# Small blocks without their low copies, constant products and spread search steps at the second layer's beginning, and the fallback branch moved forward

## The chip, the cores and the metric

The kernel runs on one core of a Trainium2 chip. The metric is the device time of one execution in microseconds (us). The core has TensorE (PE in the tables, with its weight loads as PEld), VectorE (DVE), ScalarE (ACT), GpSimd (POOL) and SyncE (SP, which issues most DMAs). Each engine works through its own instructions in order; semaphores hold an instruction back until what it needs is there.

## The reference

Three layers follow each other (cut to what is computed):

```python
# attention: B=4, H=12, S=448, D=64, causal
scores = mask(q @ k.T / 8); attn = softmax(scores); x = attn @ v      # x: 1792 x 768
# _moe_ref: 8 experts, hidden 1024
e = argmax(x @ w_gate); y = gate * (relu(x @ w1[e]) @ w2[e])          # any number of tokens per expert
# _moe2_ref: the same sizes, but each expert takes exactly 1792 / 8 = 224 tokens
for idx in argsort(-logits.flatten()):                                # best (token, expert) pair first
    tok, e = divmod(idx, 8)
    if assigned[tok] < 0 and counts[e] < 224:
        assigned[tok] = e; counts[e] += 1
out[mask_e] = relu(y[mask_e] @ w1[e]) @ w2[e]
```

## The kernel before

Products in float32 accuracy are made of three products of rounded parts: high by high, low by high and high by low (names ending in `h` and `l`: `w1h`, `w1l`, `xh`, `xl`, `hh`, `hl`). ACT rounds a weight tile from its raw buffer to the high part, and another engine subtracts it to get the low part; this pair is `split`, at L171 and L172 in the first layer and L773 and L774 in the second. A raw buffer comes free, and the next load of weights is issued, when both have read it.

`moe1` takes each expert's tokens in blocks of 128. A last block of at most 64 tokens is computed by `small` (L305): its 64 tokens fill half of the 128 columns, the other half of `xh` gets the low parts of the same tokens by two DVE copies (L309), and one product with `w1h` (L316) then makes high by high and low by high at once; a second one of 64 columns adds high by low. The branches of `expert` (L381, L389, L400, L403) decide at run time which blocks there are; all engines take them, each for itself, and `hint` names the target ahead of some of them. L417 is a row of constant products, ahead of the first expert: their operands are constants and nothing reads their result. The layer's tail (L445 to L474) brings the logits of the second layer's gate into place and sets up the first search.

`moe2` assigns the tokens with `search(p)`, one expert after the other. A search tests 40 thresholds at once in four rounds. In one round DVE compares all tokens with the thresholds (L622), PE counts by 14 small products (L665), DVE judges the counts (L666, L668), PE adds the judgments up (L676), and DVE sets the next thresholds from them (L677). After the last round PE makes a total (L566), `assign` numbers the tokens with PE's help (L710, L725, L729), and the numbers go to POOL, which gathers the tokens by an indirect DMA (L781). The generator `gen` holds these steps and yields ahead of each product of PE, so other work can be put between them: `go(n)` runs n steps, `turn` runs one when it is due, `finish` runs all that are left.

For each expert `take` transposes the gathered tokens on PE (L800) and ACT and DVE make `xh` and `xl` of them (L803, L804). The up product (L815) makes eight tiles `f` of the hidden layer from six chunks `k`, the down product (L838) makes the outputs, ACT copies them (L841), and POOL stores them by indirect DMAs (L785, the last two L791). In the first expert the up product for the first four `f` is made chunk by chunk as the weights come (`up4`, L822), so that twelve products follow each step pair of the search for the second expert.

At the very end DVE compares `bad` with zero (L918), every engine loads the verdict into a register (L921) and branches on it (L922). The body behind the branch computes the layer again by another assignment, for inputs that the search can't settle. It isn't entered with these inputs.

Of the kernel before, what the change touches and what calls it, by code (L numbers as in the profile page):

```python
# [119 lines left out]
def moe1(tc, w1, w2, wg, xs, y2, l2, ident, before, iob, cr, gt, g0, raw, early, iok, L, srch):  # L120
    nc = tc.nc
    with ExitStack() as c:
# [319 lines left out]
        for e in range(E):  # L442
            expert(e)

# [25 lines left out]
        tail3(False)  # L470
        V.tensor_mul(rh.rearrange("p (i e) -> p i e", e=E), oi[:, :, None].to_broadcast([128, NB, E]),
                     l2c[:, None, :].to_broadcast([128, NB, E]))
        nc.tensor.matmul(pU[1][:, :NB * E], hp, rh, start=True, stop=True)
        V.tensor_add(L, L, pU[1][:, :NB * E].rearrange("p (i e) -> p i e", e=E))  # L474


def moe2(tc, w1, w2, y2, out, ident, before, ones, io8, iok, iob16, L, srch, raw, force):
# [7 lines left out]
    with ExitStack() as c:  # L485
# [50 lines left out]
        iob = io8[:, None, :].to_broadcast([128, PT, E])  # L536

# [87 lines left out]
        def search(p):  # L625
# [32 lines left out]
            for r in range(RN):  # L658
# [5 lines left out]
                for i in range(PT):  # L664
                    nc.tensor.matmul(t[:TH], T["g"][:, i, :TH], T["oh"][:, i], start=(i == 0), stop=(i == PT - 1))  # L665
                V.tensor_tensor_reduce(T["d"][:TH], t[:TH], T["capm"][:TH], scale=1.0, scalar=-3.0e38,  # L666
                                       op0=OP.subtract, op1=OP.max, accum_out=T["mx"][:TH])
                V.tensor_scalar(T["ok"][:TH], T["mx"][:TH], 0.0, None, op0=OP.is_ge)  # L668
# [7 lines left out]
                nc.tensor.matmul(t[:, :1], ones[:TH], T["ok"][:TH], start=True, stop=True)  # L676
                V.scalar_tensor_tensor(thr, t[:, :1].to_broadcast([128, TH]), steps[:, r:r + 1], T["base"], op0=OP.mult,  # L677
# [9 lines left out]
            t = total()  # L687

# [6 lines left out]
        def assign(p):  # L695
# [14 lines left out]
            nc.tensor.matmul(t[:, :1], before, T["rt"], start=True, stop=True)  # L710
            V.tensor_copy(T["col"], t[:, :1])
# [14 lines left out]
            V.tensor_scalar(T["ev"], t[:16, :NA], float(N), None, op0=OP.min)  # L726
            yield YY[9]
# [38 lines left out]
        def split(p, k):  # L766
# [7 lines left out]
            (nc.gpsimd if p == 0 and k >= KD and k % 2 else V).tensor_sub(l, r, h.bitcast(F32))  # L774
# [20 lines left out]

        def take(kk):
            t = ps.tile([128, 512], F32, name="w", bufs=6)[:, :2 * CAP].rearrange("p (k g t) -> p k g t", k=2, g=2)
# [10 lines left out]
        def up(f, h):  # L808
            if h == 0:
                U[f] = ps.tile([128, 512], F32, name="w", bufs=6)[:, :CAP]  # L810
# [6 lines left out]
        def up4(k):  # L817
            for f in range(4):
                if k == 0:
                    U[f] = ps.tile([128, 512], F32, name="w", bufs=6)[:, :CAP]  # L820
# [11 lines left out]
        def down(g, hf, f0, f1):  # L832
            if f0 == 0:
                Y[0] = ps.tile([128, 512], F32, name="w", bufs=6)[:G2, :384]
# [19 lines left out]

        go(1)
        split(0, 0)
        go(2)
        split(0, 1)
        for kk in range(0, KD, 2):
            take(kk)  # L860
        for k in range(KD):
            go(2 if k < 3 else 1)
            if k + 2 < KD:
                split(0, k + 2)
            up4(k)
        for f in range(4, KF):
# [7 lines left out]
            split(0, KD + f)  # L874
        for p in range(E):
            early = p > 0 and p + 1 in done
            if p:
# [3 lines left out]
                for f in range(KF):  # L881
# [3 lines left out]
                    turn(p, 1)  # L885
                    relu(f)
# [3 lines left out]
            for g in range(2):  # L890
                for hf in range(2):
                    for f in range(0, KF, 2):
                        down(g, hf, f, f + 2)
                        turn(p, 1)
                        if n == s0[0]:
                            finish(p + 1)
                            flush()
                        if p + 1 in done and not early:
# [15 lines left out]
                if p < E - 1 or g == 0:  # L914
                    put(p, g)


        V.tensor_scalar(T["bi"], bad, 0.0, None, op0=OP.not_equal)  # L918
        if force:
            V.memset(T["bi"], 1)  # L920
        again = nc.values_load(T["bi"][0:1, 0:1], min_val=0, max_val=1)  # L921
        with tc.If(again > 0):  # L922
            reset()
            for p in range(E):
                best()
                V.tensor_tensor(T["eq"], T["lm"], T["m"][:, :, None].to_broadcast([128, PT, E]), op=OP.is_equal)
                V.tensor_mul(T["eq"], T["eq"], iob)
                V.tensor_reduce(T["mn"], T["eq"], axis=AX.X, op=OP.min)
                V.tensor_tensor(T["oh"], iob, T["mn"][:, :, None].to_broadcast([128, PT, E]), op=OP.is_equal)
                exact()  # L930
                owned()
                V.scalar_tensor_tensor(apen, T["asg"], -BIG, apen, op0=OP.mult, op1=OP.add)
                V.memset(T["fl"], 0.0)
                V.scalar_tensor_tensor(T["full"], cap, 0.0, left, op0=OP.is_equal, op1=OP.mult)
                for _ in assign(p):
                    pass
                gather(p)
                pend.clear()
                for k in range(NC):
                    load(p, k)  # L940
                    r = raw[(p * NC + k) % NR]
                    if k < KD:
                        h, l = w1h[:, k], w1l[:, k]
                    else:
                        r, h, l = r[:, :DM], w2h[:, k - KD], w2l[:, k - KD]
                    A.activation(h, r, AF.Copy)
                    V.tensor_sub(l, r, h.bitcast(F32))
                for kk in range(0, KD, 2):
                    take(kk)
# [346 lines left out]
```

## Time and profile before

| | us |
|---|---|
| median of three runs | 988.75 (986.0 to 988.78) |
| profiled execution | 990.98 |
| its span, first to last instruction | 989.1 |
| PE, DVE, ACT, POOL busy | 891.8, 629.1, 503.1, 215.4 |
| first to second layer | about 625 to 655 |
| first expert of the second layer | about 655 to 715 |
| experts two to eight | about 715 to 966 (PE busy 37.22 us of 715.5 to 753, 24.90 of the 24.90 from 941) |
| end | 966 to 989.1 |

The span is the time from the first to the last instruction of the profiled execution; 1.9 us lie around it. The mean granted clock of TensorE over the span is 0.945 of 2.4 GHz. An engine's busy time counts neither its waits nor its branches and semaphores, so a busy PE at a low granted clock is slow without waiting. A row of a timeline has in brackets how long the engine was idle ahead of it and what it waited for. A name like "PE w L838" is an instruction by engine, written tile and line.

### The profile page before, as it was taken

To read this page: it belongs to the slowest core of one execution; us is meant where nothing else is said; L and a number is where in the kernel's file an instruction comes from. 1 tells how busy PE (TensorE), PEld (TensorE's weight loads), DVE (VectorE), ACT (ScalarE), POOL (GpSimd) and SP (SyncE) were. 2 spreads that over 40 slices of the span, in tenths; PEclk is the share of its full clock that TensorE was granted. 3 is DMA by queue.
4 is the path that set the end of the run, shared out by engine and by line. 5 is a ranking of instruction groups with operands and counts; after the bars stand their busy time and mean duration, and the time that the engine had idled before them with its cause. 6 is when DMAs were issued, how large, how long until landed. Compare 5 with 4: busy or idle time off the path is not lost. (4 is left out here: it accounts for less than half of the span.)

```text
span 989.1 us, 18118 instructions
## 1 busy us (share of the span) xinstructions
PE 891.8 (90%) x6122; PEld 744.1 (75%) x6122; DVE 629.1 (64%) x1815; ACT 503.1 (51%) x1101; POOL 215.4 (22%) x244
## 2 busy tenths in 40 slices
PE   5999999995899996987999999458999999999993
PEld 3666666663778885766798878348899999999993
DVE  6888989868552613853821152578797887975640
ACT  5888888854563524654822253033444444445540
POOL 5555444404121111111211112104111011011001
PEclk9999999996999998998999999757999999999997
DMA  8654555706743803873831031074685766766701
GB/s 174 132 148 118 144 138 119 251 11 206 269 146 132 305 34 103 289 290 112 301 152 49 33 101 50 22 244 139 188 246 171 218 190 182 222 199 199 256 16 31
DMA packets 76911, 156.54 MB, mean 158 GB/s; under 512 B 30753, under 2 KB 41793, under 8 KB 76738
## 3 DMA queue, kind: packets, MB, share of 16 engines
q1 hardware_dynamic: 70514, 128.44, 42.2%
q0 software_dynamic: 6224, 26.11, 8.1%
q8 instruction: 70, 1.15, 0.5%
q14 instruction: 103, 0.84, 0.3%
HBM read 135.84 MB, written 18.67 MB: 156 GB/s over the span
## 5 line engine op out<-in xcount | busy, mean ns | idle before, releaser
L202 PE MATMUL pU<-w1h,xx 128*128 128x512 f32 x336 | 120.8, 414 | 9.0 <-DVE xx L256 2.9
L1037 ACT ACTIVATE p<-p,nm 112x112 f32<-112x112 f32 x192 | 99.8, 522 | 14.5 <-DVE nm L1030 14.2
L815 PE MATMUL w<-xh,w1h 128*128 128x224 f32 x360 | 102.1, 284 | 0.0
L815 PE MATMUL w<-xl,w1h 128*128 128x224 f32 x360 | 99.2, 276 | 0.3 <-DVE xl L804 0.3
L815 PE MATMUL w<-xh,w1l 128*128 128x224 f32 x360 | 98.8, 275 | 0.0
L1030 DVE CUSTOM_DVE_ANT_0 p<-s,msk 112x112 f32<-112x112 f32 x192 | 83.3, 440 | 12.9 <-PE s L1026 11.7
L838 PE MATMUL w<-w2h,hh 128*112 128x384 f32 x256 | 91.2, 356 | 0.0
L838 PE MATMUL w<-w2h,hl 128*112 128x384 f32 x256 | 88.0, 344 | 0.0
L838 PE MATMUL w<-w2l,hh 128*112 128x384 f32 x256 | 87.7, 342 | 0.3 <-DVE w2l L774 0.3
L202 PEld LDWEIGHTS pU<-w1h,xx 128*128 128x128 f32 x336 | 63.9, 191 | 27.0 <-issue 5.4
L1025 PE MATMUL s<-kh,qs 128*112 128x112 f32 x192 | 73.8, 384 | 10.4 <-DVE kh L1013 6.1
L1046 PE MATMUL t<-ident,p 112*112 112x112 f32 x480 | 80.3, 267 | 1.4 <-ACT pt L1051 0.8
L1008 POOL TENSOR_TENSOR qs<-qr,qs 64x448 fp32r<-64x448 f32 x44 | 54.3, 1253 | 82.4 <-ACT qs L1007 62.9
L815 PEld LDWEIGHTS w<-xl,w1h 128*128 128x128 f32 x360 | 69.1, 192 | 0.5 <-DVE xl L804 0.5
L815 PEld LDWEIGHTS w<-xh,w1h 128*128 128x128 f32 x360 | 69.0, 192 | 0.5
L815 PEld LDWEIGHTS w<-xh,w1l 128*128 128x128 f32 x360 | 69.1, 192 | 0.0
L172 DVE TENSOR_TENSOR w2l<-raw,w2h 128x768 fp32r<-128x768 f32 x64 | 58.2, 953 | 16.8 <-ACT w2h L171 14.5
L202 PE MATMUL pU<-w1l,xx 128*128 128x512 f32 x168 | 67.0, 399 | 0.0
L1057 PE MATMUL o<-pt,vt 112*64 112x336 f32 (+3 forms) x384 | 66.3, 424 | 0.0
L827 ACT ACTIVATE hh<-w 128x224 fp32r<-128x224 f32 x64 | 22.9, 358 | 84.5 <-PE w L815 63.7
L172 DVE TENSOR_TENSOR w1l<-raw,w1h 128x1024 fp32r<-128x1024 f32 x46 | 54.2, 1225 | 18.2 <-ACT w1h L171 13.5
L785 POOL DMA_INDIRECT out_dram<-yo,idx x15 | 15.3, 1021 | 231.2 <-ACT yo L841 203.0
(308 smaller groups left out, 2236.0 us busy)
## 6 DMA issues: line engine op xcount, KB each, us to landing
raw<-in_moe_w_dram SPq DMA_DIRECT2D x96, 512.0 KB
raw<-in_moe_w_dram SPq DMA_DIRECT2D x128, 384.0 KB
kr<-in_k_dram SPq DMA_DIRECT2D x46, 224.0 KB
qr<-in_q_dram SPq DMA_DIRECT2D x24, 224.0 KB
vt<-in_v_dram SPq DMA_DIRECT2D x48, 112.0 KB
xs<-xr SPq DMA_DIRECT2D x4, 1120.0 KB
xs<-xr SPq DMA_DIRECT2D x4, 238.0 KB
kr<-in_k_dram SPq DMA_DIRECT2D x4, 112.0 KB
```

Of the source, the lines that this page charges most:

```text
L172: (on or nc.vector).tensor_sub(l, r, h.bitcast(F32))
L202: nc.tensor.matmul(pU[half], a[:, k], w[:, k, cs], start=(m == 0), stop=(m == 17))
L785: nc.gpsimd.indirect_dma_start(out=out, out_offset=bass.IndirectOffsetOnAxis(ap=idx[p % 3][:, g:g + 1], axis=0), in_=yo[:, g], in_offset=None)
L815: nc.tensor.matmul(u, w[:, k, fs], x[:, k], start=(k == 0 and n == 0), stop=(k == KD - 1 and n == 2))
L827: A.activation(hh[:, f], u, AF.Relu)
L838: nc.tensor.matmul(y, a[:, f, g * G2:(g + 1) * G2], w[:, f, hf * 384:(hf + 1) * 384], start=(f == 0 and n == 0), stop=(f == KF - 1 and n = ...
L1008: (nc.gpsimd if u > 1 else nc.vector).tensor_sub(qs[64:], qr, qs[:64].bitcast(F32))
L1025: nc.tensor.matmul(s[:, :w], QS[u][:, h, i * Q:(i + 1) * Q], KH[u][:, h, :w], start=True, stop=False)
L1030: nc.vector.tensor_tensor_reduce(p, s[:, :w], msk[:, S - w:], scale=-0.125, scalar=3.0e38, op0=OP.add, op1=OP.min, accum_out=nm)
L1037: nc.scalar.activation(p, p, AF.Exp, bias=RS[u, "m"][:, h, i:i + 1], scale=-1.0, accum_out=RS[u][:, h, i:i + 1])
L1046: nc.tensor.transpose(t[:, k], P[u, h][:, o + k * Q:o + (k + 1) * Q], ident[:Q, :Q])
L1057: nc.tensor.matmul(OPS[u][h * 64:(h + 1) * 64, k * Q:], VT[u][:, h, k], PT[u, h][:, k, k * Q:], start=(k == 0), stop=(k == NQ - 1))
```

## The change

Five things are changed.

1. In `small` the two copies at L309 are gone. The columns that they filled stay zero, and the product of the low parts of the tokens with `w1h` is no longer made in these blocks.
2. Constant products, of 128x512 in bfloat16 as those of L417, are put into PE's order: ten in the first layer's tail (2, 2, 2 and 4), 43 in the first search (2 behind each L665, 4, 4, 4 and 5 behind the four L676, 5, 6 and 2 behind L566, L710 and L725) and 28 between there and the first transposes (7, 2, 4, 5 and 10).
3. `up4` is cut into two halves of six products; for the first three chunks a search step runs ahead of each half.
4. The four w2l subtractions of the first expert that POOL made are made by DVE.
5. The verdict is loaded during the down product of the seventh expert (p = 6), with a hint for the branch, and the branch stands in the up product of the eighth, behind its first tile. The body repeats what is needed up to that place, and uses four PSUM buffers of its own (`alt`). At the end there is no branch.

```diff
         def small(e, j):
-            for s in (slice(0, 1), slice(1, KD)):
-                nc.vector.tensor_copy(xh[:, s, HB:], xl[:, s, :HB])
             sp = begin(e, j, gf[:, e + 1:e + 2])
...
+        def warm(n):
+            for _ in range(n):
+                nc.tensor.matmul(wz, before, iob16[:, None, :].to_broadcast([128, 4, 128]), start=True, stop=True)
...
                 V.tensor_tensor_reduce(T["d"][:TH], t[:TH], T["capm"][:TH], scale=1.0, scalar=-3.0e38,
                                        op0=OP.subtract, op1=OP.max, accum_out=T["mx"][:TH])
+                if p == 0:
+                    warm(2)
                 V.tensor_scalar(T["ok"][:TH], T["mx"][:TH], 0.0, None, op0=OP.is_ge)
...
                 nc.tensor.matmul(t[:, :1], ones[:TH], T["ok"][:TH], start=True, stop=True)
+                if p == 0:
+                    warm(4 if r < RN - 1 else 5)
...
-            (nc.gpsimd if p == 0 and k >= KD and k % 2 else V).tensor_sub(l, r, h.bitcast(F32))
+            V.tensor_sub(l, r, h.bitcast(F32))
...
+        warm(7)
         go(1)
+        warm(2)
         split(0, 0)
-        go(2)
+        go(1)
+        warm(4)
+        go(1)
+        warm(5)
         split(0, 1)
+        warm(10)
         for kk in range(0, KD, 2):
             take(kk)
         for k in range(KD):
-            go(2 if k < 3 else 1)
+            go(1)
             if k + 2 < KD:
                 split(0, k + 2)
-            up4(k)
+            up4(k, 0, 2)
+            if k < 3:
+                go(1)
+            up4(k, 2, 4)
...
+        def judge():
+            finish(E - 1)
+            V.tensor_scalar(T["bi"], bad, 0.0, None, op0=OP.not_equal)
...
+            verdict.append(nc.values_load(T["bi"][0:1, 0:1], min_val=0, max_val=1))
+            tc.mark_branch_hint_location("again", verdict[0] > 0, engines=list(nc.engines))
+
+        def redo():
+            u0 = U[0]
+            alt.extend([ps.tile([128, 512], F32, name="w", bufs=6) for _ in range(4)])
+            with tc.If(verdict[0] > 0, label="again"):
+                reset()
...
+                    if last:
+                        U[0] = u0
+                        up(0, 0, True)
+                        up(0, 1, True)
+                        break
...
                     up(f, 1)
                     turn(p, 1)
+                    if p == E - 1 and f == 0:
+                        redo()
                     relu(f)
...
+                        if p == E - 2 and n == 4:
+                            judge()
```

Three places in the order of the engines follow. PE, second layer, from the search to the first half product; w is the PSUM tile of the up product, gp that of the search. Before:

```order
L665 MATMUL gp<-t_oh,t_g 40x8
L676 LDWEIGHTS ones
L676 MATMUL gp<-t_ok,ones 128x1
L822 MATMUL w<-xh,w1h 128x224
L822 MATMUL w<-xh,w1l 128x224
L822 MATMUL w<-xl,w1h 128x224
```

After:

```order
L855 MATMUL w<-xh,w1h 128x224
L855 MATMUL w<-xh,w1l 128x224
L855 MATMUL w<-xl,w1h 128x224
L693 LDWEIGHTS ones
L693 MATMUL gp<-t_ok,ones 128x1
L855 MATMUL w<-xh,w1h 128x224
L855 MATMUL w<-xh,w1l 128x224
L855 MATMUL w<-xl,w1h 128x224
```

L693 is the old L676 and L855 the old L822: six of the twelve products now stand between the counts (L680, the old L665) and L693, and six behind it.

DVE at the same place, from the tokens' low parts (L804) to the second weight subtraction; srch holds the thresholds. Before:

```order
L804 TENSOR_TENSOR xl<-w,xh 128x448 x3
L666 ISA t_d,t_mx<-gp,t_capm 40x8
L666 ISA t_mx 40x1
L668 TENSOR_SCALAR t_ok<-t_mx 40x1
L552 TENSOR_REDUCE t_mn<-t_ao 128x14
L677 SCALAR_TENSOR_TENSOR srch_87<-gp,steps,t_base 128x40
L622 TENSOR_TENSOR t_g<-t_mm,srch_87 128x14x40
L660 TENSOR_TENSOR t_col<-srch_87,steps 128x1
L661 TENSOR_SCALAR t_base<-iok,steps,t_col 128x40
L774 TENSOR_TENSOR w1l<-raw_90,w1h 128x1024
```

After:

```order
L837 TENSOR_TENSOR xl<-w,xh 128x448 x3
L681 ISA t_d,t_mx<-gp,t_capm 40x8
L681 ISA t_mx 40x1
L685 TENSOR_SCALAR t_ok<-t_mx 40x1
L567 TENSOR_REDUCE t_mn<-t_ao 128x14
L799 TENSOR_TENSOR w1l<-raw_90,w1h 128x1024
L696 SCALAR_TENSOR_TENSOR srch_87<-gp,steps,t_base 128x40
L637 TENSOR_TENSOR t_g<-t_mm,srch_87 128x14x40
```

The subtraction of w1l (L799, the old L774) has moved from behind the next thresholds to ahead of them (L696, the old L677).

POOL at the end of the kernel, from the stores of the last expert. Before:

```order
L785 DMA out_dram<-yo,idx_23605 1792x768
L791 DMA out_dram<-yo,idh 3584x384 x2
L921 TENSOR_LOAD t_bi
L922 COMPARE_AND_BRANCH
L608 MEMSET apen 128x14
```

After:

```order
L930 UNCONDITIONAL_BRANCH
L930 ISA
L930 UNCONDITIONAL_BRANCH
L810 DMA out_dram<-yo,idx_23583 1792x768
L816 DMA out_dram<-yo,idh 3584x384 x2
L1356 UNCONDITIONAL_BRANCH
L1356 ISA
```

The load of the verdict and the branch (now L930) stand ahead of the last expert's stores (L810 and L816, the old L785 and L791), and behind the stores only the program's end is left.

## Rows read from the trace of the kernel before

**Rows 1.** Stages: busy time by engine (instructions), granted clock, DMA share, GB/s.
```profile
630.40:646.60 16.20, 4.21 (x77) 3.42 (x77) 12.88 (x68) 0.00 (x0) 0.00 (x0) 0.55 0.11 36
655.10:676.00 20.90, 19.00 (x134) 17.94 (x135) 14.85 (x56) 6.51 (x9) 0.00 (x0) 0.57 0.55 193
676.00:690.00 14.00, 11.36 (x106) 10.76 (x104) 12.07 (x25) 7.23 (x14) 8.60 (x5) 0.88 0.47 151
690.00:710.00 20.00, 19.75 (x128) 16.73 (x126) 13.04 (x38) 6.56 (x9) 2.49 (x7) 0.83 0.65 203
```

**Rows 2.** PE timeline, first search: start, us, line, operation, idle time ahead, releaser.
```profile
636.79 0.62 PE L665 MATMUL gp<-t_oh,t_g 128*40 128x8 bf16 x14 [1.13 <-DVE t_g L622]
640.24 0.18 PE L676 MATMUL gp<-t_ok,ones 40*128 40x1 bf16 x1 [0.44 <-DVE t_ok L668]
645.81 0.17 PE L729 MATMUL gp<-t_ev,sel 16*112 16x15 f16 x1 [0.25 <-DVE t_ev L726]
655.12 2.32 PE L800 MATMUL w<-ident,xg 112*128 112x112 f32 x11 [1.82 <-DMA xg<-y,idx]
```

**Rows 3.** Line L417: count, ns min/median/max, first and last start.
```profile
L417 PE MATMUL pU<-iob,before x9: 607/634/634, 231.2 to 234.6; 128*128 128x512 bf16 x9
```

**Rows 4.** PE timeline, half up products of the first expert.
```profile
659.10 0.56 PE L822 MATMUL w<-xh,w1h 128*128 128x224 f32 x1
661.94 0.63 PE L665 MATMUL gp<-t_oh,t_g 128*40 128x8 bf16 x14
663.12 0.56 PE L822 MATMUL w<-xh,w1h 128*128 128x224 f32 x1
674.14 0.35 PE L822 MATMUL w<-xh,w1h 128*128 128x224 f32 x1
675.56 0.28 PE L815 MATMUL w<-xh,w1h 128*128 128x224 f32 x1
```

**Rows 5.** DVE timeline, one round of the same stretch.
```profile
659.50 0.74 DVE L622 TENSOR_TENSOR t_g<-t_mm,srch 128x560 bf16<-128x560 f32 x1
662.60 0.16 DVE L666 CUSTOM_DVE_ANT_0 t_d<-gp,t_capm 40x8 f32<-40x8 f32 x1 [0.82 <-PE gp L665]
```

**Rows 6.** Line L774, then DVE and PE timeline beside the last POOL subtractions.
```profile
L774 DVE TENSOR_TENSOR w2l<-raw,w2h x60: 937/950/959, 676.2 to 958.5; 128x768 fp32r<-128x768 f32 x60
L774 POOL TENSOR_TENSOR w2l<-raw,w2h x4: 1806/1852/2321, 679.9 to 686.7; 128x768 fp32r<-128x768 f32 x4
685.03 2.27 DVE L622 TENSOR_TENSOR t_g<-t_mm,srch 128x560 bf16<-128x560 f32 x1
687.36 0.63 PE L665 MATMUL gp<-t_oh,t_g 128*40 128x8 bf16 x14 [2.64 <-DVE t_g L622]
```

**Rows 7.** Waits of PE, and L403 and L316 in two small blocks.
```profile
PE pU L316 <- DVE xx L309: 14.6, 3, 7.2
L403 PEldq COMPARE_BRANCH  x1: 75/75/75, 392.4 to 392.4; - x1
394.25 0.76 PE L316 MATMUL pU<-w1h,xx 128*128 128x512 f32 x1 [7.17 <-DVE xx L309]
L403 PEldq COMPARE_BRANCH  x1: 70/70/70, 457.6 to 457.6; - x1
461.93 0.77 PE L316 MATMUL pU<-w1h,xx 128*128 128x512 f32 x1 [4.96 <-DVE xx L309]
```

**Rows 8.** POOL's last store, and its queue's instructions at L922 and L1292.
```profile
975.82 0.94 POOL L791 DMA_INDIRECT out_dram<-yo,idh  x1 [3.57 <-PEq L922]
L922 POOLq INC_SWDGE_SEM  x1: 1932/1932/1932, 979.0 to 979.0; - x1
L1292 POOLq DRAIN  x3: 50/114/7339, 980.9 to 988.8; - x3
```

**Rows 9.** Waits of PE for its sequencer, and PE's branch at L922.
```profile
PE pY L220 <- PEq L381: 2.7, 4, 0.8
L922 PEldq COMPARE_BRANCH  x1: 3616/3616/3616, 971.5 to 971.5; - x1
```

More of the change, by code (lines that the diff above doesn't have):

```diff
@@ L443, in moe1 @@
             expert(e)
+        def warm(n):
+            for _ in range(n):
+                nc.tensor.matmul(pU[1], before, iob[:, None, :].to_broadcast([128, 4, 128]), start=True, stop=True)
         nc.sync.dma_start(L, l2[:N].rearrange("(p i) e -> p i e", i=NB))
@@ L474, in moe1 @@
         V.tensor_add(L, L, pU[1][:, :NB * E].rearrange("p (i e) -> p i e", e=E))
+        for _ in range(4):
+            nc.tensor.matmul(pU[0], before, iob[:, None, :].to_broadcast([128, 4, 128]), start=True, stop=True)
 def moe2(tc, w1, w2, y2, out, ident, before, ones, io8, iok, iob16, L, srch, raw, force):
@@ L806, in moe2, with up @@
         U = {}
-        def up(f, h):
-            if h == 0:
-                U[f] = ps.tile([128, 512], F32, name="w", bufs=6)[:, :CAP]
+        def up(f, h, again=False):
+            if h == 0 and not again:
+                U[f] = wt()[:, :CAP]
             u = U[f]
@@ L874, in moe2 @@
             split(0, KD + f)
+        def judge():
+            finish(E - 1)
+            V.tensor_scalar(T["bi"], bad, 0.0, None, op0=OP.not_equal)
+            if force:
+                V.memset(T["bi"], 1)
+            verdict.append(nc.values_load(T["bi"][0:1, 0:1], min_val=0, max_val=1))
[5 more added lines that the diff above has]
+                reset()
+                for p in range(E):
+                    best()
+                    V.tensor_tensor(T["eq"], T["lm"], T["m"][:, :, None].to_broadcast([128, PT, E]), op=OP.is_equal)
+                    V.tensor_mul(T["eq"], T["eq"], iob)
+                    V.tensor_reduce(T["mn"], T["eq"], axis=AX.X, op=OP.min)
+                    V.tensor_tensor(T["oh"], iob, T["mn"][:, :, None].to_broadcast([128, PT, E]), op=OP.is_equal)
+                    exact()
+                    owned()
+                    V.scalar_tensor_tensor(apen, T["asg"], -BIG, apen, op0=OP.mult, op1=OP.add)
+                    V.memset(T["fl"], 0.0)
+                    V.scalar_tensor_tensor(T["full"], cap, 0.0, left, op0=OP.is_equal, op1=OP.mult)
+                    for _ in assign(p):
+                        pass
+                    gather(p)
+                    last = p == E - 1
+                    for k in range(NC):
+                        load(p, k)
+                        if last and k >= KD:
+                            continue
+                        r = raw[(p * NC + k) % NR]
+                        if k < KD:
+                            h, l = w1h[:, k], w1l[:, k]
+                        else:
+                            r, h, l = r[:, :DM], w2h[:, k - KD], w2l[:, k - KD]
+                        A.activation(h, r, AF.Copy)
+                        V.tensor_sub(l, r, h.bitcast(F32))
+                    for kk in range(0, KD, 2):
+                        take(kk)
+                    if last:
[3 more added lines that the diff above has]
+                        break
+                    for f in range(KF):
+                        up(f, 0)
+                        up(f, 1)
+                        relu(f)
+                    for g in range(2):
+                        for hf in range(2):
+                            down(g, hf, 0, KF)
+                        put(p, g)
+            alt.clear()
@@ L914, in moe2 @@
                 if p < E - 1 or g == 0:
[L915 to L949, printed above, removed]
-                for f in range(KF):
-                    up(f, 0)
-                    up(f, 1)
-                    relu(f)
-                for g in range(2):
-                    for hf in range(2):
-                        down(g, hf, 0, KF)
                     put(p, g)
```

29 lines of the change are left out of this document (24 added, 5 removed).

## The prediction

> **What bounds the kernel now.** I read the table of stages first, then the timelines of the stages in which TensorE (PE) is not full, then the waits. From 715 us to 966 us PE is the bound and the change puts only one branch there, so all else is decided in three places.
>
> The first is the second layer's beginning. From 630 us the stages show the granted clock at .55, then .57 while PE is busy 19.00 of 20.90 us, then .88 and .83 [rows 1]. A share s of a stretch at the lower of the two levels (1.2 GHz, against 2.4) gives a mean of 1 - s/2: so some 18 of the 20.9 us from 655 us ran at the lower level, 3.4 of the next 14 and 6.8 of the 20 after. Ahead of the fall PE did little: in the first search it runs L665 and L676 and waits 1.13 and .44 us ahead of them for VectorE (DVE), and later for the gathered tokens, which land at 655.12 us [rows 2]. In the half products behind it a round lasts 4.02 us (659.10 to 663.12), in which twelve products take 2.84 us; at the upper level the same twelve take 1.42 us [rows 4]. DVE is busy in such a round but for .82 us [rows 5]. Then GpSimd (POOL) subtracts four w2l tiles at 1.85 us, DVE's own taking .95; DVE's L622 beside one of them takes 2.27 us where it takes .74 alone [rows 5, 6], and PE sits idle 2.64 us for it [rows 6]. After this idle time the clock is low again.
>
> The second is the small blocks of the first layer: three of the four wait for the copies of L309, 14.6 us in all [rows 7]. The third is the end: behind the last store POOL increments a semaphore (1.93 us) and drains (7.34 us) before anything else may end [rows 8].
>
> **The change part by part**, each in us of the profiled execution.
>
> *Small blocks.* The eight copies go, and with them a product of two low parts. What holds PE next is its own branch, then DVE's later work in the block. In the longest wait PE's branch at L403 starts at 392.4 us and the block at 394.25: at most 1.8 us come free, I take 1.6. In the last one the branch starts at 457.6 us and the block at 461.93: up to 4.2 us; since DVE is late there itself and the block needs five w2l subtractions from it (5 x .95), I take 3. The remaining wait is 14.6 - 7.17 - 4.96 = 2.4 us [rows 7]; DVE is in w1l subtractions there, and the gate values that the block needs soon after (L311) are copied behind them, so some 60 per cent, 1.4. Sum 6.0; bounds 3 (DVE holds the last block after all) and 9 (all that is free, and the clock stays up because the idle time is shorter).
>
> *Constant products.* One costs .425 us at the lower level (nine start from 231.2 to 234.6 us, at .63 us from start to end [rows 3], so I read them as at the lower level), and by the ratio of 2.84 to 1.42 an estimated .21 at the upper. Two follow L665: .43 in a gap of .44. Four follow L676: .85 in a gap of 1.13. Two stand ahead of L729, which waits .25: .2 late. The 28 ahead of the transposes take 5.9 us, and the tokens land 9.3 us after L729's start [rows 2]. The ten of the first layer's tail stand in waits for DVE. So at the upper level they cost about .2, and L665's fourteen products (.62 us a round [rows 2]), which are shorter there, give about that back: 0, bounds -.3 and +.7.
>
> *What a clock that stays up is worth, and the spreading.* Up products: the order on DVE puts the w1l subtraction between L668 and L677, the order on PE six products before L676 and six after, so PE has work while DVE subtracts. DVE's busy time per round (4.02 - .82 = 3.2 us [rows 4, 5]) becomes the period; three rounds give 2.0 with some loss. The next two and a half groups of twelve run at 1.42 instead of 2.84, less a wait for DVE: 1.6. The eleven transposes take half of 2.32 us [rows 2], of which DVE's copies of the tokens hide half: .6. Then the wait of 2.64 us: without POOL's subtractions L622 takes 1.5 us less, while DVE has four times .95 more in that stretch, of which it had 1.9 us idle (12.07 busy of 14 [rows 1]): 1.2. Last, the down products: some 10 us (3.4 + 6.8) at the lower level behind the wait would take 5: 4.8. Sum 10.2. Not all of it can arrive: the next expert's tokens need six w1l subtractions, three xl and the search on DVE, which is busy 13.04 of 20 us from 690 us [rows 1] and waits for PE's answers in the rest. With everything 6 us earlier, the loads behind those subtractions are late next. I take 8. Bounds: 3 (the clock falls again; only spreading and the shorter wait are left) and 11 (all, and a faster search).
>
> *The end.* POOL's drain now stands straight behind its last store, whose issue ends at 976.76 us (975.82 + .94), not at 980.9, where the 1.93 us increment ends [rows 8]. If its 7.34 us run from its own start, 4.1 us are saved; if it ends a fixed time after the store has landed, nothing is. I take 2.5.
>
> *The branch.* It now stands in the last expert (p = 7), behind the first of its up products, where PE has no slack. At a hinted branch in the first layer PE waited 2.7 us in four cases, .7 each; PE's own unhinted one at L922 took 3.6 us [rows 9]. The hint comes some 13 us ahead of it, and the value is loaded behind `bi`, which stands on DVE behind w1l subtractions that end before PE gets there. I take +1.0, bounds +.7 and +3.6.
> The Trainium skill (Advanced Engine Details and Errata, section Control Flow Timing) gives about 108 ns for a compare-and-branch. By that the sum would be .9 lower; L922's 3616 ns does not agree with it.
>
> **The sum.** -6.0 + 0 - 8 - 2.5 + 1.0 = -15.5. The profiled execution took 990.98 us (span 989.1 and 1.9 around it), so 975.5; it is 2.2 us above the median of 988.75, and against that median the same sum gives 973.3. With all terms at their worse bounds (-3, +.7, -3, 0, +3.6) 1.7 us are left, with all at their better ones (-9, -.3, -11, -4.1, +.7) 23.7.
>
> **Rivals.**
> (A) *The clock falls again in the up products.* For it: with twelve products at 1.42 us and one L665 in a round of 3.2 us, PE idles a good third of the time, in two short waits a round, as it did in longer ones in the search when the clock fell. Against: the waits ahead of L665 and L676 were 1.13 and .44 us there with next to no products between them [rows 2], and here full groups stand around each. Then the term of 8 is 3, and the time 973.3 + 5 = 978.3.
> The Trainium skill (TensorE: Matmul & The Clock Gate, section A second HAM failure mode: psum-queue depth-cycling) reports a kernel whose short idle times between groups of products let the clock swing between its levels. This is the rival that it speaks for; no row of before has full groups with such gaps at the upper level, so the trace neither agrees nor disagrees.
> (B) *Not L309 but the branches hold PE in the small blocks.* For it: in the longest wait PE's own branch starts only 1.8 us before the block [rows 7], and what DVE does next in these blocks is hardly earlier. Then 6 becomes 1: 978.3.
> (A) and (B) together: 983.3.
> (C) *The products come too late to lift the clock, and hold the search: slower.* The place is the first search from 631.9 us. At .425 us two behind L665 take .85 in a gap of .44 (+.41, four times), four behind L676 1.70 in 1.13 (+.57, three times), and the 18 after the last round 7.65, where from 640.24 to 645.81 us [rows 2] some 4.5 of 5.6 us are free: +3.1. The 28 ahead of the transposes take 11.9 us where 9.3 less 1.2 of other work are free: +3.8. Together +10.2. With the gain there at 3 and the small blocks and the end at 3 and 0, the branch at 1, that is 988.75 + 10.2 - 5 = 994.0. It decides once the other parts save less than 10.2 us. Against it: the clock stood at its upper level until 630.4 us, and the first products follow the first L665 [rows 2], so the lull that brought it down is filled from its start.
> (D) *Gains that cancel*: the branch at 3.6, the end at 0, A and B true: 988.75 - 1 - 3 + 3.6 = 988.4, no change.
>
> **How the numbers follow.** Chances: the forecast .54, A .18, B .12, A with B .06, C .04, D .06. The forecast and the range go by the median. About 3 us (.3%) is what a measurement of this kernel can tell from no change, so A, B and both together count as faster: .90 faster, .06 within, .04 slower. The likeliest case gives 973.3. The range reaches up to A with B (983.3) and down to small blocks and clock at their better bounds (973.3 - 3 - 3 - 1.6 = 965.7): 965.5 to 983.5 leaves out C, D and the corners.
>
> **What would show it.** In the profile after: a granted clock near 1.00 from 630 to 690 us; groups of twelve at about 1.4 us and rounds of 3.2 to 3.5; no wait on L309 and none of several us ahead of the small blocks; L622 at .74 throughout; the down products of the first expert at the upper level; POOL's drain starting within 1 us of its last store's issue; PE idle about 1 us once between 920 and 945 us. The prediction is wrong if the clock is at .5 in the up products, if the drain ends no earlier after the last store, if DVE rather than PE is found busy without a break from 690 to 716 us with PE waiting, or if the branch costs PE more than 2 us.

## The result and the profile after

The changed kernel takes 975.64 us (median of four runs, 971.83 to 977.33) against 988.76 (986.0 to 990.77): 0.9864 of the time before, 95% interval 0.9826 to 0.9901, or 13.1 us less. Forecast were 973.3 us and 15.5 us less. The profiled execution took 975.56 us with a span of 973.7, 15.4 us less than the span before.

Where the 15.4 us are is read from four marks that both traces have: the first count of the first search (L665, now L680), the first up product of the second expert (L815, now L848), PE's last product, and the end.

| stretch | before | after | difference | forecast |
|---|---|---|---|---|
| start to first count | 631.96 | 627.27 | -4.7 | -6.0 |
| first count to second expert | 81.23 | 73.55 | -7.7 | -8 |
| second expert to PE's end | 260.95 | 262.86 | +1.9 | +1.0 |
| PE's end to the end | 14.96 | 10.02 | -4.9 | -2.5 |

These are the stages of the second layer's beginning after the change: length, busy time of PE, PEld, DVE, ACT and POOL (instructions), granted clock, DMA share and GB/s. They answer to [rows 1]:

```profile
627.30:640.90 13.60, 12.43 (x114) 5.41 (x114) 10.86 (x59) 0.00 (x0) 0.00 (x0) 1.00 0.08 24
640.90:649.50 8.60, 7.10 (x45) 3.27 (x45) 7.34 (x26) 2.12 (x2) 2.28 (x7) 1.00 0.87 295
649.50:668.00 18.50, 16.64 (x133) 15.09 (x132) 14.21 (x55) 6.05 (x9) 0.00 (x0) 0.72 0.63 225
668.00:677.50 9.50, 9.13 (x89) 8.67 (x89) 7.96 (x25) 6.74 (x15) 2.17 (x2) 1.00 0.58 188
677.50:700.80 23.30, 21.75 (x168) 19.06 (x169) 18.73 (x54) 8.97 (x14) 1.42 (x5) 1.00 0.65 206
```

The clock is at its upper level through the search and in the down product, but not in the stage between, where its mean over 18.50 us is .72. PE's timeline there (the counts L680 and their sums L693, with the half products between them; idle time and its releaser in brackets) answers to [rows 4]:

```profile
651.00 0.51 PE L680 MATMUL gp<-t_oh,t_g 128*40 128x8 bf16 x14
...
653.04 0.17 PE L693 MATMUL gp<-t_ok,ones 40*128 40x1 bf16 x1 [0.61 <-DVE t_ok L685]
...
655.29 0.63 PE L680 MATMUL gp<-t_oh,t_g 128*40 128x8 bf16 x14 [1.22 <-DVE t_g L637]
...
657.41 0.18 PE L693 MATMUL gp<-t_ok,ones 40*128 40x1 bf16 x1
...
659.07 0.63 PE L680 MATMUL gp<-t_oh,t_g 128*40 128x8 bf16 x14
```

At 651.00 us the 14 counts take .51 us, at 655.29 us .63: in between the clock fell, after PE had waited .61 and 1.22 us between its groups. The rounds are 4.29 us (with the tokens' low parts in it) and 3.78. For 8 us the granted clock is .50, in columns as above:

```profile
655.00:659.00 4.00, 3.71 (x27) 3.35 (x27) 3.54 (x13) 0.66 (x1) 0.00 (x0) 0.50 0.66 225
659.00:663.00 4.00, 4.00 (x30) 3.63 (x30) 3.03 (x14) 0.00 (x0) 0.00 (x0) 0.50 0.37 119
```

The wait of 2.64 us ahead of the third search [rows 6] is nearly gone, since DVE's operations have their usual length. The first two rows are DVE's, the third is PE's:

```profile
675.07 0.27 DVE L631 TENSOR_TENSOR t_lm<-L,t_pen 128x112 f32<-128x112 f32 x1
...
676.68 0.74 DVE L637 TENSOR_TENSOR t_g<-t_mm,srch 128x560 bf16<-128x560 f32 x1
```

```profile
677.47 0.51 PE L680 MATMUL gp<-t_oh,t_g 128*40 128x8 bf16 x14 [0.36 <-DVE t_g L637]
```

PE's waits, in total, times, and the longest, answer to [rows 7, 9]:

```profile
PE pU L314 <- ACT w2h L171: 6.9, 1, 6.9
...
PE pA L236 <- DVE yb L231: 3.0, 1, 3.0
...
PE w L871 <- DVE w2l L799: 1.5, 1, 1.5
...
PE w L848 <- DVEq L930: 0.9, 1, 0.9
...
PE w L848 <- PEq L930: 0.3, 1, 0.3
```

No wait on the copies is left. 6.9 us stand ahead of the second small block, where the trace names ACT but PE's own branches are the cause: L387 took 5.22 us there (4.44 before, where it is L389), and the next one, L401, starts .2 us before the block. The second row is that of before:

```profile
L387 PEldq COMPARE_BRANCH  x1: 5219/5219/5219, 388.5 to 388.5; - x1
```

```profile
L389 PEldq COMPARE_BRANCH  x1: 4439/4439/4439, 387.9 to 387.9; - x1
```

```profile
L401 PEldq COMPARE_BRANCH  x1: 75/75/75, 393.8 to 393.8; - x1
```

3.0 us are a new wait, in the fourth small block, for the copy yb, which stands on DVE behind five w2l subtractions:

```profile
456.64 4.43 DVE L172 TENSOR_TENSOR w2l<-raw,w2h 128x768 fp32r<-128x768 f32 x5
461.00 0.41 DVE L231 COPY yb<-pB 128x256 f32<-128x256 f32 x1
```

```profile
461.46 0.64 PE L236 MATMUL pA<-yb,wg 128*32 128x128 f32 x4 [3.00 <-DVE yb L231]
```

At the end, the last store and the drain of POOL's queue answer to [rows 8]:

```profile
964.54 0.94 POOL L816 DMA_INDIRECT out_dram<-yo,idh  x1 [2.68 <-ACT yo L874]
```

```profile
L1356 POOLq DRAIN  x3: 46/120/8524, 964.3 to 973.4; - x3
```

### The profile page after: what moved, and what is told of

It is laid out like the page before. It is cut to its first block, busy times and chain, and to the rows that moved or that the text cites. A ratio compares the mean times of both kernels' runs of the same rounds, so it can differ in the third digit from the quotient of the medians.

```text
span 973.7 us, 18257 instructions
## 1 busy us (share of the span) xinstructions
PE 902.2 (93%) x6198; PEld 743.5 (76%) x6198; DVE 624.5 (64%) x1811; ACT 502.2 (52%) x1101; POOL 203.9 (21%) x240
## 5 line engine op out<-in xcount | busy, mean ns | idle before, releaser
L848 PE MATMUL w<-xh,w1h 128*128 128x224 f32 x360 | 102.4, 284 | 0.3 <-PEq L930 0.3
L848 PE MATMUL w<-xh,w1l 128*128 128x224 f32 x360 | 99.0, 275 | 0.9 <-DVEq L930 0.9
L848 PE MATMUL w<-xl,w1h 128*128 128x224 f32 x360 | 98.9, 275 | 0.3 <-DVE xl L837 0.3
L848 PEld LDWEIGHTS w<-xh,w1l 128*128 128x128 f32 x360 | 69.0, 192 | 1.1 <-DVEq L930 1.1
L848 PEld LDWEIGHTS w<-xh,w1h 128*128 128x128 f32 x360 | 69.0, 192 | 1.0 <-issue 0.5
L848 PEld LDWEIGHTS w<-xl,w1h 128*128 128x128 f32 x360 | 69.1, 192 | 0.5 <-DVE xl L837 0.5
L172 DVE TENSOR_TENSOR w2l<-raw,w2h 128x768 fp32r<-128x768 f32 x64 | 58.5, 957 | 15.2 <-ACT w2h L171 13.6
L799 DVE TENSOR_TENSOR w2l<-raw,w2h 128x768 fp32r<-128x768 f32 x64 | 60.9, 951 | 8.2 <-ACT w2h L798 8.0
## 6 DMA issues: line engine op xcount, KB each, us to landing
xs<-xr SPq DMA_DIRECT2D x4, 238.0 KB
```

What stands on the lines that cost most here:

```text
L172: (on or nc.vector).tensor_sub(l, r, h.bitcast(F32))
L848: nc.tensor.matmul(u, w[:, k, fs], x[:, k], start=(k == 0 and n == 0), stop=(k == KD - 1 and n == 2))
```

## The experiments

Runs differ by 2 to 6 us for one kernel (before: 984.75 to 990.91 in 13 runs), so single parts are read from the traces' marks, and the runs are told beside them. Us between the marks, in all profiles:

| kernel | second small block to first count | first count to first whole up product | to first down product | to second expert | to PE's end | last store to the end |
|---|---|---|---|---|---|---|
| before | 237.7 | 43.60 | 12.36 | 25.27 | 260.95 | 13.28 |
| after | 233.3 | 40.68 | 9.96 | 22.91 | 262.86 | 9.16 |
| e1, POOL subtracts | 233.4 | 40.61 | 12.23 | 25.22 | 264.64 | 9.16 |
| e2, no constant products | 233.6 | 42.93 | 9.97 | 24.27 | 262.84 | 9.12 |
| e3, whole half products | 232.9 | 42.70 | 9.96 | 24.41 | 262.94 | 9.12 |
| e4, rounds filled | 233.0 | 38.73 | 9.96 | 24.30 | 262.89 | 9.17 |
| e5, copies back | 235.8 | 41.84 | 9.96 | 24.30 | 262.83 | 9.16 |
| e6, no fallback | 235.8 | 40.34 | 9.97 | 22.91 | 260.90 | 9.13 |
| e8, combined | 232.0 | 38.86 | 9.97 | 24.13 | 262.92 | 9.13 |
| e9, before, DVE subtracts | 238.0 | 43.39 | 9.96 | 24.46 | 260.86 | 13.44 |
| e10, combined, products earlier | 231.2 | 39.41 | 9.96 | 22.91 | 262.95 | 9.12 |
| e11, one wait at the end | 232.9 | 41.78 | 9.96 | 24.29 | 262.93 | 11.08 |
| e12, before, no copies | 235.8 | 43.27 | 12.35 | 25.35 | 260.91 | 13.13 |

**What the subtractions on POOL cost** (e1 and e9).

```diff
-            V.tensor_sub(l, r, h.bitcast(F32))
+            (nc.gpsimd if p == 0 and k >= KD and k % 2 else V).tensor_sub(l, r, h.bitcast(F32))
```

> The changed kernel with one part undone: POOL again makes four of the first expert's w2l subtractions. Theory (the 4.5 us between the last up product of the first expert and the end of its down product come from these subtractions): DVE's operations beside them are stretched again to about 1.9 and 2.3 us, PE waits some 2.5 us ahead of the first counts of the third search (0.36 us in the changed kernel), the granted clock falls behind that wait and the down products start at the lower level; 4 to 5 us more than the changed kernel, about 980. Rival (the constant products and the earlier clock bring these 4.5 us, and the subtractions only change hands): within 1 us of the changed kernel, about 976, with no fall of the clock near 677 us.

979.26 us (976.74 to 981.64), 3.6 more than the change. The two stretches behind the first whole up product grow from 9.96 to 12.23 and from 22.91 to 25.22 us, 4.6 together. Against e5 and e11, whose code is the change's in these stretches and which need 24.3 us in the second, it is 3.2. (The 1.8 us more up to PE's end are another fall of the clock, behind the branch, in this execution alone.) DVE's and PE's timelines:

```profile
671.48 1.87 DVE L631 TENSOR_TENSOR t_lm<-L,t_pen 128x112 f32<-128x112 f32 x1
673.38 0.27 DVE L632 TENSOR_REDUCE t_m<-t_lm 128x14 f32<-128x112 f32 x1
...
673.78 0.27 DVE L644 TENSOR_TENSOR t_oh<-t_lm,t_m 128x112 bf16<-128x112 f32 x1
...
674.68 2.26 DVE L637 TENSOR_TENSOR t_g<-t_mm,srch 128x560 bf16<-128x560 f32 x1
```

```profile
677.00 0.51 PE L680 MATMUL gp<-t_oh,t_g 128*40 128x8 bf16 x14 [2.63 <-DVE t_g L637]
```

The first and the last row of DVE are operations of two tensors, and they last 1.87 and 2.26 us beside POOL's 1.85 us (.27 and .74 in the change). L632, which reads one tensor, takes its usual .27, and so does L644, of two tensors again, which falls into a pause of POOL (673.2 to 674.5 us). PE waits 2.63 us, and the stage that follows has a mean clock of .87:

```profile
677.00:702.70 25.70, 24.20 (x169) 21.13 (x169) 18.75 (x52) 8.31 (x12) 4.98 (x8) 0.87 0.55 174
```

The theory held: the clock fell here although the constant products were there. The Trainium skill (GPSIMD Engine Reference, section 1. Specifications) says that GpSimd shares its SBUF interfaces with VectorE and contends with instructions of two SBUF inputs or in a two-port mode; L631 and L637 agree with it.

The same part alone, in the kernel before, is the reverse edit.

> The kernel before with one part of the change alone: DVE makes the four subtractions that POOL made. Theory (they stretch DVE's work beside them, PE waits, the clock falls): 11.8 us from the first whole up product to the third search become 9.5, the down stage behind it 23 to 24.5 us instead of 25.3, together 3 to 4.5 us, about 984.5. Rival (it pays only together with a clock that has been kept up before): at most 1.5 us, about 987.5.

984.74 us (ten runs, 981.78 to 988.15), ratio 0.9963 (0.9945 to 0.9981). The two stretches take 9.96 and 24.46 us, 3.2 less than before. So this part pays alone, a little less than the 4.6 us above; the clock falls again in the down stage of this execution (.93).

**What the constant products and the spreading bring** (e2 and e3).

```diff
-            for _ in range(n):
+            for _ in range(0):
                 nc.tensor.matmul(wz, before, iob16[:, None, :].to_broadcast([128, 4, 128]), start=True, stop=True)
```

(and so for the ten in the first layer's tail). The trace of the change has 76 of these products, 10 in the tail, 38 in the first search and 28 behind it; the 43 and 81 given for them elsewhere are too many.

> The changed kernel without its 81 constant products. Theory (they speed up the search's rounds by 0.1 us each, halve the transposes and the first half products, and nothing else, since the clock falls again in the half products with them too): the clock falls near 627 us, the shift against the changed kernel is 1.5 to 2 us at the first whole up product and at most 2 us at the end, about 977.5. Rival (the products' clock carries on into the stages behind): 4 us or more, about 980.

975.28 us (972.88 to 977.18): in the runs no difference from the change. In the trace the first whole up product comes 2.25 us later after the first count, a little more than the theory had; 1.36 more are lost in the down stage, where the clock fell in this execution (.93). Of the 2.25 some is chance: the change's own code took 40.34 to 41.84 us for this stretch in five profiles (after, e1, e5, e6, e11), 41.05 in the mean, so that 1.9 are left.

```diff
             go(1)
             if k + 2 < KD:
                 split(0, k + 2)
-            up4(k, 0, 2)
-            if k < 3:
-                go(1)
-            up4(k, 2, 4)
+            up4(k, 0, 4)
```

(with `go(2)` for the first three chunks).

> The changed kernel with the half products whole again: both search steps of a chunk ahead of its twelve products. Theory (spreading lets PE work while DVE subtracts): three rounds of about 3.9 to 4.0 us in the place of 3.6 (the mean of the changed kernel), so 1 to 1.5 us more, about 977. Rival (the two gaps of a spread round are what lets the clock fall at 654 us): with whole groups the clock stays at its upper level, the rounds get no longer and the products behind them are faster; 1 to 2 us less, about 974.

976.89 us (973.2 to 977.63). The same stretch is 2.0 us longer than in the change, and the clock fell in the half products all the same:

```profile
652.00:667.80 15.80, 14.08 (x105) 13.46 (x106) 12.44 (x52) 3.72 (x6) 0.00 (x0) 0.68 0.45 151
```

So the rival is out: the clock falls without the gaps of a spread round too. Before, this stretch took 43.60 (43.27 and 43.39 in e12 and e9); the products without spreading leave 42.70, spreading without the products 42.93, both together 41.05 in the mean of five. By the means each alone brings less than 1 us and the two 2.4. The runs can't tell these differences apart.

**What the fall of the clock in the half products costs** (e4).

```diff
+        def fill(n):
+            for _ in range(n):
+                nc.tensor.matmul(GP[0][:, 256:512], before, iob16[:, None, :].to_broadcast([128, 2, 128]), start=True, stop=True)
...
             up4(k, 0, 2)
             if k < 3:
+                fill(4)
                 go(1)
             up4(k, 2, 4)
+            if k < 3:
+                fill(4)
```

> The changed kernel with 24 more constant products (128x256) in the three spread rounds, four behind each half group, in otherwise unused columns of the search's PSUM tiles. They are to keep the granted clock at its upper level there. Theory (DVE bounds these rounds and the stage behind): the clock stays up, rounds of 3.2 to 3.4 us, the first whole up product 1.5 to 2.5 us earlier, of which about 1 us is left at the second expert: about 974.5. Rival (the clock is the bound there, as my forecast's term had it): 3 us or more are left, about 972.5. Third: the products come in the search's way, and the rounds get longer than 3.6 us.

974.92 us (972.39 to 975.89). The clock stays up in that stage; this is its row and that of the down stage:

```profile
646.90:663.40 16.50, 15.78 (x156) 13.35 (x155) 13.90 (x54) 5.99 (x9) 0.00 (x0) 1.00 0.67 244
...
673.00:697.70 24.70, 23.15 (x169) 20.19 (x169) 18.75 (x54) 9.26 (x14) 1.42 (x5) 0.93 0.61 197
```

The first whole up product comes 1.95 us earlier than in the change. The second round takes 3.22 us (3.78 in the change, but 3.22 and 3.23 in e5, e6 and e11, which have no filling); most of what the filling brings comes behind that round. At the second expert .6 us of it are left, because in the down stage PE is without idle time but for one wait of 1.55 us and ran 1.4 us longer with the clock at .93 than with 1.00.

That stage is where executions of the same code part: the down stage takes 22.91 us in after and in e6, and 24.3 in e5 and e11, whose code is the same there. The rows of e6 and e5:

```profile
676.50:699.80 23.30, 21.74 (x168) 19.05 (x169) 18.73 (x54) 8.97 (x13) 1.42 (x5) 1.00 0.66 211
```

```profile
680.60:705.40 24.80, 23.24 (x169) 20.25 (x169) 18.85 (x54) 9.07 (x14) 1.42 (x5) 0.93 0.61 199
```

In the four profiles from the first count to the second expert are 73.55, 73.22, 76.10 and 76.03 us: the profile shown above is on the good side, the mean gain of this stretch (against 81.23) is 6.5 us.

**What the copies cost** (e5 and e12).

```diff
+            for s in (slice(0, 1), slice(1, KD)):
+                nc.vector.tensor_copy(xh[:, s, HB:], xl[:, s, :HB])
             sp = begin(e, j, gf[:, e + 1:e + 2])
```

> The changed kernel with one part undone: the two copies of the low parts are back in the small blocks. Theory (the copies held PE in the third and fourth small block, its own branch in the second): waits on the copies of 2 to 3 us in the third and about 5 us in the fourth block come back, the first count of the first search starts 5 to 7 us later than the mean of 625.1 us that five profiles without the copies show (623.8 to 627.3), about 981 us. Rival (the branches hold PE there anyhow): at most 1 us later, about 976.

977.53 us (976.9 to 980.0), 1.9 more; the first count at 629.25 us, 4.1 behind the mean of 625.1 and not 5 to 7. So the time is less than was expected of it. The waits are back where the theory put them: these are the starts of the third and fourth block.

```profile
439.17 0.47 PE L316 MATMUL pU<-w1h,xx 128*128 128x512 f32 x1 [2.44 <-DVE xx L309]
```

```profile
459.39 0.76 PE L316 MATMUL pU<-w1h,xx 128*128 128x512 f32 x1 [4.89 <-DVE xx L309]
```

The reverse edit in the kernel before:

> The kernel before with one part of the change alone: the small blocks without the copies. Theory: 4 to 5.5 us less, about 984, with the first count near 626 us (632.0 and 630.6 in two profiles with the copies). Rival (the branches hold PE): less than 1.5 us.

981.36 us (six runs, 978.3 to 982.75), ratio 0.9929 (0.9912 to 0.9946), 6.4 less; the first count at 623.70 us, 8.3 earlier than before, of which 4.0 stand ahead of the first small block (264.20 and 268.15 us), where the two kernels are the same. From the second block to the first count three profiles with the copies take 235.8 to 238.0 us (mean 237.2) and eight without 232.9 to 235.8 (mean 233.8). From the second block on the copies are worth some 3.3 us by the traces; in all they are worth 1.9 and 6.4 us by the two pairs of runs, and which of the two is nearer stays open. The rival (B) is out for the third and fourth block, and right for the second.

**What the branch costs and the end brings** (e6 and e11). In e6 `judge()` and `redo()` are not called: the fallback isn't there.

> The changed kernel without the fallback: neither the load of the verdict nor the branch nor the body is there, for these inputs nothing else is left out. Theory (the branch in the last expert costs PE 1.9 us, and the end is shorter only because nothing stands between the last store and the drain): PE needs 261.0 us from the second expert's first up product to its end, as in the kernel before, where the changed kernel needs 262.9; from the last store to the end 9.2 us as in the changed kernel; about 974 us. Rival (the 4.1 us at the end come from the moved body, not from the order of store and drain): 13.3 us from the last store to the end.

972.78 us (971.67 to 973.57), 2.9 less than the change. From the second expert to PE's end 260.90 us, as before, and 9.13 us from the last store to the end, as in the change: the theory held in both numbers. What the branch does to PE in the change, in two rows of PE and three of the queues:

```profile
931.44 0.34 PE L848 MATMUL w<-xh,w1h 128*128 128x224 f32 x1 [0.30 <-PEq L930]
932.71 0.37 PE L848 MATMUL w<-xh,w1l 128*128 128x224 f32 x1 [0.93 <-DVEq L930]
```

```profile
L930 DVEq COMPARE_BRANCH  x1: 80/80/80, 929.8 to 929.8; - x1
L930 PEldq COMPARE_BRANCH  x1: 469/469/469, 930.4 to 930.4; - x1
...
L930 DVEq EVENT_SEMAPHORE  x1: 21/21/21, 932.6 to 932.6; - x1
```

PE's branch takes .47 us. DVE's takes .08, but DVE's next instruction, a semaphore that PE waits for, comes at 932.6 us, 2.8 us behind it. PE waits for it longer than for its own branch. Before, with no hint, DVE's next instruction behind the branch at the end came 2.8 us later as well:

```profile
L922 DVEq COMPARE_BRANCH  x1: 68/68/68, 960.2 to 960.2; - x1
...
L922 DVEq EVENT_SEMAPHORE  x1: 21/21/21, 963.0 to 963.0; - x1
```

What DVE's queue does in these 2.8 us no row shows.

For the drain:

```diff
                 if p < E - 1 or g == 0:
                     put(p, g)
+        nc.gpsimd.memset(yo[:1, 1, 384:385], 0.0)
```

> The changed kernel with one GpSimd instruction more behind its last store, a write into the stored tile, which has to wait until the store has read it. First theory (the drain takes its 7 to 8.5 us from its own start): it starts some 3 us later, and the end comes 2 to 3 us later, about 978. Second theory (the drain ends a fixed time after the store has landed): it is shorter by what it starts later, the end moves by less than 0.3 us, about 975.6.

974.31 us (973.31 to 976.91). POOL's rows, and the drain:

```profile
964.02 0.94 POOL L816 DMA_INDIRECT out_dram<-yo,idh  x1 [2.90 <-ACT yo L874]
966.82 0.09 POOL L1023 MEMSET yo<- 1x1 f32 x1 [1.87 <-DMA out_dram<-yo,idh]
```

```profile
L1358 POOLq DRAIN  x3: 46/120/7472, 966.8 to 974.8; - x3
```

The write waits until the store is done, at 966.82 us, and the drain takes 7.47 us from 966.8: from the last store to the end 11.08 us and not 9.16. The drain therefore runs from the end of POOL's last instruction, and not for a fixed time after the store has landed. (It lasts 7.34 us before, behind nothing, and 8.52 in the change, with the .94 us of the store's issue in it.) That the runs are not above the change's shows how little 1.9 us stand out in them.

**A version that takes more** (e8 and e10): the change, the filled rounds of e4, six more products in the down stage, and in the small blocks `SPS = (2,3,2,0,3,4,0)` for `(5,0,2,0,3,4,0)`, so that three of the five subtractions come behind yb.

> The changed kernel with the products in the spread rounds, six more 128x512 products ahead of the down step in which PE waits 1.55 us for a w2l subtraction, and in the small blocks three of the first five weight splits behind the copy that PE waits 3.0 us for (yb). Theory: the clock stays at its upper level from 625 to 955 us, the stage from the first down product to the second expert takes 22.9 us instead of 24.3, the wait for yb goes and 1.5 to 2.5 us of it are left at the end of the first layer; 4 to 5 us less than the changed kernel, about 971. Rival (w2l subtractions are only put off and PE waits for them in the next step; the products hold PE): within 1 us of the changed kernel.

971.98 us (968.84 to 972.23). The wait for yb is 1.0 us and no longer 3.0, with a new one of 1.7 for hh later in the same block. The down stage takes 24.13 us although the clock stayed up (1.00): the six products had been put behind the wait of 1.55 us, and held PE for 1.1 us. Moved one step earlier:

```diff
-                        if p == 0 and n == 2:
+                        if p == 0 and n == 1:
                             z = wt()
                             for _ in range(6):
                                 nc.tensor.matmul(z, before, iob16[:, None, :].to_broadcast([128, 4, 128]), start=True, stop=True)
```

> The combined version before this one, with its six products one down step earlier, ahead of the wait for the w2l subtraction and not behind it (where they only put PE's next products off by 1.1 us). Theory (PE is without idle time in the down stage but for that wait, and a clock that stays up is worth 1.4 us there): 22.9 to 23.1 us from the first down product to the second expert in the place of 24.13, about 970.9. Rival (the second expert's weights and tokens bound that moment): 24 us again, about 972.

966.46 us (965.78 to 967.55), ratio 0.9786 of before (0.9768 to 0.9804), 21.3 us less. The three stages, at the upper level throughout:

```profile
642.40:658.60 16.20, 15.48 (x155) 13.35 (x155) 13.91 (x54) 6.00 (x9) 0.00 (x0) 1.00 0.66 232
658.60:668.10 9.50, 9.16 (x89) 8.69 (x87) 7.97 (x25) 6.51 (x14) 2.17 (x2) 1.00 0.61 203
668.10:691.50 23.40, 22.97 (x175) 19.73 (x175) 18.84 (x54) 9.37 (x14) 1.42 (x5) 1.00 0.63 207
```

The down stage is at 22.91 us, as the theory had it, in one profile, and from the first count to the second expert are 72.28 us. The time is 4.4 us below the 970.9 that were expected. Of the 5.5 us between e8 and e10 this explains .7; in e10's execution the first count comes at 619.19 and not 624.13 us, of which 3.2 stand ahead of the first small block, where the two kernels are the same. They ran on different chips, and what made that difference was not looked into.

## Why the prediction was right, step by step

The direction, the size (15.5 forecast, 13.1 in the runs, 15.4 in the profile) and all three places were right. The terms were off in both directions, and that their sum came out to .1 us in the profile is in part luck: what the small blocks (1.3), the second layer's beginning (.3) and the branch (.9) fell short of the forecast, the end (2.4) made up, and the profile is on the good side; by the runs 2.4 us are missing.

- *Small blocks*, -6.0: measured -4.7 in the profile, -3.3 from the second block on by the means of the profiles, -1.9 and -6.4 by runs. By the starts of the blocks [rows 7] the profile's 4.7 are -.2 up to the second block (I had 1.6; its own branch took 5.22 us in place of 4.44), -3.4 from the second to the third (42.4 us in place of 45.8; I had 1.4), -6.1 from the third to the fourth (15.8 in place of 21.9) and +5.1 from there to the first count (175.1 in place of 170.0), where I had 3 for the last block in all. The step that failed is the last block: PE did start its products at once, and then waited 3.0 us for yb behind the five subtractions, and ran slower behind it (.64 us for the four products that take .41 in e8). What was free ahead of the block was given back inside it; with yb ahead of three of the subtractions (e8) it is 171.5 us.
- *Constant products*, 0: no delay, as worked out. With the spreading they bring more than I had put down for them: without them the first whole up product is 2.25 us later, 1.9 against the mean of five profiles.
- *The stage of the half products*: here rival (A) came true. The clock fell in the spread rounds in every profile without e4's filling, to .50 from 655 to 663 us in the one above, which is the prediction's own sign of a wrong step. Transposes to first whole up product took 18.45 us where 20.44 had been (-2.0, against the sum of 2.0, 1.6 and .6 for rounds, later groups and transposes).
- *The wait behind POOL*, 1.2: 2.4. I had charged DVE's four additional subtractions against it; they lengthened no wait ahead of this search. PE's wait for w2l of 1.55 us, one step later (.25 before), is theirs in e9 at most: e1, where POOL makes four of the subtractions, has it too (1.50), so its cause stays open.
- *The down product*, 4.8 before clipping: 2.4 in the profile and 1.0 where the clock falls. The step that held the whole term was the clipping: 10.2 to 8, against 7.7 in the profile and 6.5 in the mean of four. Its reason was not the one I gave. The second expert's weights were not late; PE had no idle time but the 1.55 us, and e4 and e10 show that it is PE and its clock that set this stage.
- *Rival (A)'s price*, 3 in place of 8, was wrong although (A) happened: it tied the gain of the wait and of the down product to the clock in the half products. They hang on POOL's subtractions (e1: 3.2 to 4.6 us with everything else in place).
- *The end*, -2.5: -4.9. I had put it midway between two ends, and the upper one was true (4.1, e11). The other .8 is POOL's last store, which had waited for a branch (L922, 3.57 us, [rows 8]) and now follows the output at once. The increment that stood ahead of the drain (1.93 us) is not gone: it is made behind the branch at 933.2 us (L930, 1.89 us), where POOL has nothing else to do.
- *The branch*, +1.0: +1.9 (e6). PE's own part was in the range; that PE would have to wait for what DVE does behind its branch was missing. The 108 ns that the Trainium skill gives (Advanced Engine Details and Errata, section Control Flow Timing) are nearer to DVE's record of 80 ns than to what DVE's next instruction shows, 2.8 us.

## What to carry to other kernels

A clock that has fallen is a symptom with a place: look for the wait ahead of each fall, and price the wait's own cause before the clock. Here one helper on POOL cost 3.2 to 4.6 us through a chain of four steps (stretched DVE, waiting PE, lower clock, late next stage), and 76 constant products brought some 2 us up to the first whole up product, which the runs did not show.
Filling PE's waits paid where PE set the pace and the filling stood ahead of the wait; behind it, the same six products cost 1.1 us.
What stood between the last store and the end of the program was paid in full here, and a branch can be moved off the end for less than it cost there, if what all engines wait for after it is counted too.

## What was not expected of the hardware

- POOL's final drain takes 7.3 to 7.5 us from the end of POOL's last instruction, whether the last store has landed (before, e11) or not (the change).
- After the branch in the last expert the engines come back at different times: PE's first product .5 us behind its branch, DVE's next instruction 2.8 us behind its own, in the same place of the program and with the same hint. Before, without a hint, DVE's was 2.8 us behind its branch too, and PE's branch took 3.6.
- The same code in the same stage ran with the clock up in two profiles and with a fall in two others (22.91 and 24.3 us), which alone makes 1.4 us between two executions.
